# The second block's projections, taken in the first block as pairs of 64-row half tiles

## The chip, the core and the metric

The kernel runs on one core of a Trainium2 chip. A core has five engines that run side by side and wait for each other by semaphores: TensorE (PE, matmuls, its weight loads shown apart as PEld), VectorE (DVE), ScalarE (ACT), GpSimd (POOL) and SyncE (SP, which here only issues DMAs). Sixteen DMA engines move data. The metric is the device time of one execution in microseconds. Before the change it is 217.17 us, the median of 3 runs (216.95 to 217.29).

## What is computed

A sequence of 2048 rows of width 448, normalized once, goes through a sliding-window attention (16 heads of 28, window 256) and, in parallel, through a gated feed-forward part (width 1792). Both results are added to the input.

```python
xn = _layernorm(x)
# attention
q, k, v = split(xn @ wqkv)                 # 16 heads of 28
scores  = q @ k.T * 28 ** -0.5             # masked: 0 <= i - j < 256
a       = softmax(scores) @ v @ wo
# feed-forward
b       = (gelu(xn @ w_gate) * (xn @ w_up)) @ w_down
out     = x + a + b
```

## The kernel before

**Blocks and stages.** The 2048 rows are worked off in four blocks of 512 (`qb` 0 to 3), each of four tiles of 128 rows. A block has an attention stage (`attention`, L560) and a gate stage (`gated`, L451); the down projection of a block (`gen_down`) is done inside the attention stage of the next one. In the first block the attention stage has nine steps (`steps_of`, L502). A step issues four-head score matmuls on PE (`sc`, L632), one exponential over 128x2048 on ScalarE (L638), the masks on GpSimd, and then what its entry in `plan` says. At the start of the steps with index 4, 6 and 8 there is a pass of probabilities times v (`pv`, L591, tile `ov`).

**The plan.** `plan` (L778) is an order written out by hand: a list for each step. `(u, n)` takes n pieces of work from the generator `u`, one piece being between one and seven matmuls; a function is called as it stands. All engines' instructions are issued in this order, each engine works its own off in order, and SP issues its DMAs in this order too. So where a function that issues DMAs stands in the plan decides where these stand on SP.

**What the first block's plan holds.** `gen_qk` makes the first block's own q and k of head groups 1 to 3. `gen_up(0, ...)` makes up-projection pairs 1, 2 and 3 ahead of the gate stage (tile `ue`; a pair is 14 matmuls of 64x512 in seven slots of two at a time, then two casts on VectorE). `gen_v(4, ..)`, `gen_v(6, ..)` and `gen_qk_next` make the second block's v, q and k: six 128-row matmuls and two 64-row halves for each pair of results (`v_dense`, `v_half`, `proj`, `qk_halves`), so 7 slots. `q_last` makes q of head group 3 with four 128-row matmuls. The gate stage begins with up pair 0 (`up(0)`, tile `u`) and gate 0 (tile `gt`).

**Half tiles and swapped copies.** The width of 448 is 3.5 times 128. Up and gate projections, and in blocks 2 and 3 also the projections (`gen_pairs`, L343), use pairs of 64-row matmuls: one on the array's rows 0 to 63, the other on rows 64 to 127, at the same time, seven chunks of 64 each. For every second chunk the data must lie in the other half of the partitions. Three tensors hold such swapped copies: `xsw` of the normalized rows (a ring for two blocks, filled by `swap(qb)`, L409), `wvs` of the v weights and `wsq` of the q and k weights (filled by `swap_weights`, L415). Before, `swap(1)` and both `swap_weights` stand at the start of the second block (L797 to L800), where only the second block's gate stage and the projections for blocks 2 and 3 need them.

**Normalization.** `stat(t)` takes mean and variance of a tile on VectorE, `rstd(t, n)` makes the deviations of n tiles with two small activations on ScalarE, `norm(t)` writes the normalized tile `xn` (448 columns, and again 64 columns as a second copy of the last half chunk) and `dma_transp(t)` transposes it by DMA into `xnT`. For tiles 5, 6 and 7 the 64 columns are GpSimd's (L167). `rstd(5, 3)` stands in the third step right before the exponential, behind that step's q copy (L636).

**Loads.** `ahead()` (first step) transposes tile 4 and loads part of `wu` and `wg`; `ahead3()` (third step) normalizes and transposes tiles 5 to 7 and then, by `loads()`, loads the rest of `wu`, `x_sb`, the rest of `wg`, `wo` and `wd`, all on SP. `fill_pads(False)` in the fourth step completes the weights `wqp` and `wkp` on GpSimd; `wsq` is a copy of these.

**PSUM banks.** Projections, up pairs and `ov` share four banks (`take` and `give`, L203): the one that was given back first is taken next. A bank is free once the copy out of it is done. The scores have a pool of their own.

Of the kernel before, what the change touches and what calls it, by code (L numbers as in the profile page):

```python
# [17 lines left out]
P = 128  # L18
# [8 lines left out]
def kernel(  # L27
# [136 lines left out]
    def norm(t):  # L164
        xn = work.tile([P, 4, P], bf16, name="xn", bufs=4)
        xf = xn[:, :, :].rearrange("p a b -> p (a b)")
        both = ((nc.vector, 0, D, 0), (nc.gpsimd if t in (5, 6, 7) else nc.vector, D, 64, 384))  # L167
        for eng, lo, n, src in both if t > 3 else both[:1]:
            eng.tensor_scalar(out=xf[:, lo:lo + n], in0=x_sb[:, t, src:src + n], scalar1=mv_all[:, t, 0:1],
                              scalar2=rstd_all[:, t:t + 1], op0=ALU.subtract, op1=ALU.mult)  # L170
        xns[t] = xn
# [47 lines left out]
    def v_dense(t, pv):  # L219
        mm3(pv, lambda c: xnT[:, c, t * P:(t + 1) * P], lambda c: wv[:, c, :], True, False)  # L220
# [4 lines left out]
    def v_copy(t, pv, copy):  # L225
        copy(out=v_sb[:, t, :, 0:Dh], in_=pv.rearrange("p (h d) -> p h d", d=Dh))
        give(pv)

    def gen_v(t, scalar):

        two = [None, None]
        for i in range(2):
            two[i] = take("pv", D)
            v_dense(t + i, two[i])
            yield 570
        for i in range(2):
            v_half(t + i, two[i])
        for i in range(2):
            v_copy(t + i, two[i], nc.vector.tensor_copy if i and not scalar else nc.scalar.copy)
        yield 360  # L240

# [81 lines left out]

    def gen_qk_next():

        pairs = []
        for g, parts, end in ((0, "qk", None), (1, "q", 0), (1, "k", None), (3, "", 1), (2, "qk", 2)):
            for part, w in (("q", wqp), ("k", wkp)):
                if part in parts:
                    ps = take("p" + part)  # L330
                    proj(ps, w, 1, g)
                    pairs.append(ps)
                    yield 650
            if g == 3:
                q_last(1)
                yield 870
            if end is not None:
                two, pairs = pairs[:2], pairs[2:]
                qk_halves(1, end, *two)
                qk_copies(1, end, *two)  # L340
                yield 360

    def gen_pairs(qb):  # L343

# [26 lines left out]

        return chain(v_pair(4 * qb), qk_pair(0), v_pair(4 * qb + 2), qk_pair(1), qk_pair(2))

# [186 lines left out]
    def attention(qb, plan):  # L560
# [54 lines left out]
        for i, (scores, ncol, edges) in enumerate(steps):  # L615
# [12 lines left out]
            for g, half, kt, q0, nq, col in scores:  # L628
# [9 lines left out]
            nc.scalar.activation(out=p_sb[:, :, 0:ncol], in_=ss[:, :, 0:ncol], func=ACT.Exp, scale=SCALE)  # L638
# [101 lines left out]
    def ahead():  # L740
        norm(4)
        dma_transp(4)
        load_ffn(wu, B_w_up, slice(0, 1))
        load_ffn(wg, B_w_gate, slice(0, 3))

    def ahead2():
        stat(6)
        stat(7)

    def ahead3():  # L750
        for t in (5, 6, 7):
            norm(t)
            dma_transp(t)
        loads()

    def loads():

        load_ffn(wu, B_w_up, slice(4, 7))
        nc.sync.dma_start(out=x_sb[:, 12:16, :], in_=xv[:, 12:16, :])
        load_ffn(wg, B_w_gate, slice(3, 7))  # L760
        wo_v = A_wo.rearrange("(g j d) n -> j d g n", g=4, j=4)
        for j in range(4):
            nc.sync.dma_start(out=wo[32 * j:32 * j + Dh, :, :], in_=wo_v[j])
        for k in range(0, NF, 4):
            n = min(4, NF - k)
            nc.sync.dma_start(out=wd[:, k:k + n, :], in_=rows(B_w_down, k, n))

    for qb in range(NB):
# [4 lines left out]
        if qb == 0:  # L773
            new_hT(0)
            early = (1, 2, 3)
            u = chain(gen_qk((1, 2, 3), {1: (3, pvs[3]), 2: (2, pvs[2])}), gen_up(0, (1, 2)), gen_v(4, False), gen_up(0, (3,)),
                      gen_v(6, True), gen_qk_next())
            plan = [[(u, 2), ahead, (u, 1)], [lambda: v_dense(2, pvs[2]), (u, 2), ahead2, (u, 1)], [lambda: spare.append(spare.pop(1)), (u, 2), ahead3, (u, 4)],  # L778
                    [(u, 11), lambda: fill_pads(False)], [lambda: stat(8), (u, 10), lambda: fill_pads(True)], [(u, 3)],
                    [lambda: stat(9), (u, 4)], [lambda: stat(10), (u, 3)], [lambda: stat(11), (u, 3), lambda: rstd(8, 4)]]  # L780
        else:
            d = gen_down(qb - 1)
            if qb < 3:
                u = gen_pairs(qb + 1)
                plan = [[(d, 14)], [(d, 11)], [(d, 11)], [(u, 7)], [(d, 18)], ["sums", (u, 7), "inverse"], [(u, 12)],
# [189 lines left out]
```

## Time and profile before

| | us |
|---|---|
| median of 3 runs | 217.17 |
| the profiled execution | 217.4 |
| its span, first to last instruction | 215.7 |
| first block, attention steps (scores of the first to up pair 0) | 11.6 to 37.0 |
| first block, gate stage | 37.0 to 54.8 |
| DMA moved in the span | 15.21 MB |

How to read the lines: a row of the timeline or of the chain has the start in us, the duration in us, engine, source line, operation, output and inputs, and in brackets the idle time before it and what ended it. PE's matmuls overlap, so durations of single ones are longer than the distance of their starts, and the distance tells the rate. A row of SP is the issue of a DMA, not its transfer. A row of waits has who waited for whom, us in total, how often, and the longest. A row of a stretch has its bounds and length, then each engine's busy time with its count, the granted clock, the share of the DMA engines and GB/s.

### The profile page before, as it was taken

To read this page: it belongs to the slowest core of one execution; us is meant where nothing else is said; L and a number is where in the kernel's file an instruction comes from. 1 tells how busy PE (TensorE), PEld (TensorE's weight loads), DVE (VectorE), ACT (ScalarE), POOL (GpSimd) and SP (SyncE) were. 2 spreads that over 40 slices of the span, in tenths; PEclk is the share of its full clock that TensorE was granted. 3 is DMA by queue.
4 is the path that set the end of the run, shared out by engine and by line. 5 is a ranking of instruction groups with operands and counts; after the bars stand their busy time and mean duration, and the time that the engine had idled before them with its cause. 6 is when DMAs were issued, how large, how long until landed. Compare 5 with 4: busy or idle time off the path is not lost.

```text
span 215.7 us, 6281 instructions
## 1 busy us (share of the span) xinstructions
PE 209.6 (97%) x2687; PEld 101.7 (47%) x2692; DVE 156.7 (73%) x348; ACT 132.0 (61%) x125; POOL 48.0 (22%) x81
## 2 busy tenths in 40 slices
PE   7999999999999999999999999999999999999993
PEld 2433333444445445544445445544444444444793
DVE  7896779799456997588547799567359699687721
ACT  4698589645876976613777697423578676467000
POOL 5286968520000202022000012022000020205001
PEclk9999999999999999999999999999999999999999
DMA  6999499913391000102330000200000000000001
GB/s 195 267 241 184 80 231 226 300 30 69 78 251 51 24 3 27 18 3 50 70 97 24 24 0 3 58 9 3 0 3 22 26 3 24 21 3 0 21 29 49
DMA packets 23553, 15.21 MB, mean 71 GB/s; under 512 B 9856, under 2 KB 23264, under 8 KB 23520
## 3 DMA queue, kind: packets, MB, share of 16 engines
q1 hardware_dynamic: 22576, 14.47, 27.9%
q8 instruction: 22, 0.36, 0.6%
q10 hardware_dynamic: 944, 0.29, 0.5%
q14 instruction: 11, 0.09, 0.2%
HBM read 8.69 MB, written 2.18 MB: 50 GB/s over the span
## 4 chain that ended last, share of the span: by engine, by line
PE 92%; DMA 2%; DVE 2%; ACT 1%; issue 1%; POOL 1%; DVEq 0%; POOLq 0%; ACTq 0%
PE po L391 26%; PE gt L431 20%; PE u L431 14%; PE sc L632 6%; PE ue L431 5%; PE ov L599 5%; PE pq L365 4%; PE pv L351 3%; PE pq L190 3%; PE pv L190 2%; PE pk L190 2%; DMA xnT<-xn 1%; DMA x_sb<-in_A_x_dram 1%; ACT p_sb L638 1%; DVE st L154 1%
## 5 line engine op out<-in xcount | busy, mean ns | idle before, releaser
L638 ACT ACTIVATE p_sb<-sc 128x2048 bf16<-128x2048 f32 x39 | 73.3, 1878 | 20.6 <-PE sc L632 13.8
L566 POOL TENSOR_TENSOR oN<-oc,l 128x512 bf16<-128x512 f32 x16 | 22.2, 1387 | 140.3 <-DVE l L579 140.3
L470 ACT ACTIVATE ge<-gt 128x1024 bf16<-128x1024 f32 x28 | 28.7, 1024 | 39.1 <-PE gt L431 33.8
L391 PE MATMUL po<-wd,hT 128*128 128x448 bf16 (+1 forms) x266 | 47.9, 324 | 0.0
L431 PE MATMUL gt<-xnT,wg 64*128 64x512 bf16 x224 | 45.4, 376 | 0.0
L431 PE MATMUL gt<-xsw,wg 64*128 64x512 bf16 x168 | 40.6, 376 | 0.0
L478 DVE TENSOR_TENSOR hT<-ge,u 128x512 bf16<-128x512 bf16 x38 | 24.4, 680 | 17.9 <-PE u L431 10.1
L547 DVE TENSOR_TENSOR p_sb<-p_sb,masks 128x256 bf16<-128x256 bf16 (+1 forms) x90 | 30.1, 390 | 5.9 <-ACT p_sb L638 5.9
L391 PEld LDWEIGHTS <-hT 128*128 128x128 bf16 x266 | 24.6, 98 | 16.0 <-issue 1.0
L431 PE MATMUL u<-xnT,wu 64*128 64x512 bf16 x152 | 31.7, 376 | 0.0
L431 PEld LDWEIGHTS <-wg 64*128 64x128 bf16 x392 | 19.6, 94 | 21.9 <-issue 0.2
L431 PEld LDWEIGHTS <-wu 64*128 64x128 bf16 x392 | 19.0, 94 | 23.0 <-issue 3.3
L431 PE MATMUL u<-xsw,wu 64*128 64x512 bf16 x114 | 27.2, 376 | 0.0
L399 DVE TENSOR_TENSOR res<-po,x_sb 128x448 bf16<-128x448 f32 (+1 forms) x17 | 10.1, 593 | 18.8 <-PE po L391 18.8
L632 PE MATMUL sc<-qT,kT 28*64 28x320 bf16 (+7 forms) x648 | 16.4, 261 | 0.3 <-ACT p_sb L638 0.2
L557 POOL TENSOR_SCALAR_AFFINE_SELECT p_sb<-p_sb 128x512 bf16<-128x512 bf16 (+1 forms) x21 | 14.3, 707 | 4.7 <-ACT p_sb L638 4.6
L431 PE MATMUL ue<-xnT,wu 64*128 64x512 bf16 x72 | 15.1, 377 | 0.0
L391 PE MATMUL po<-wo,oN 128*128 128x448 bf16 (+1 forms) x76 | 15.1, 323 | 0.0
L447 DVE CAST hT<-ue 128x512 bf16<-128x512 f32 x18 | 11.5, 682 | 2.9 <-PE ue L431 2.9
L632 PEld LDWEIGHTS <-kT 28*64 28x64 bf16 (+1 forms) x648 | 7.7, 102 | 12.6 <-issue 10.9
L431 PE MATMUL ue<-xsw,wu 64*128 64x512 bf16 x54 | 13.5, 377 | 0.0
L572 DVE STREAM_TRANSPOSE l<-oc 128x512 f32<-128x512 f32 x16 | 11.3, 704 | 1.6 <-POOL oN L566 1.6
(103 smaller groups left out, 251.7 us busy)
## 6 DMA issues: line engine op xcount, KB each, us to landing
out_dram<-res SPq DMA_DIRECT2D x15, 112.0 KB
xsw<-xnT SPq DMA_DIRECT2D x8, 192.0 KB
x_sb<-in_A_x_dram SPq DMA_DIRECT2D x3, 448.0 KB
wu<-in_B_w_up_dram SPq DMA_DIRECT2D x4, 336.0 KB
wd<-in_B_w_down_dram SPq DMA_DIRECT2D x3, 448.0 KB
wg<-in_B_w_gate_dram SPq DMA_DIRECT2D x2, 448.0 KB
wg<-in_B_w_gate_dram SPq DMA_DIRECT2D x2, 336.0 KB
wraw<-in_A_wqkv_dram SPq DMA_DIRECT2D x2, 252.0 KB
```

Source lines behind the costliest of these rows:

```text
L190: nc.tensor.matmul(ps, lhsT=lhs(c), rhs=rhs(c), start=start and c == 0, stop=stop and c == 2, skip_group_check=True)
L391: nc.tensor.matmul(po[:, a:b], lhsT=x[:, k, cs], rhs=wt[:, k, lo + a:lo + b], start=(n == a == 0), stop=(n == len(terms) - 1), skip_group_ ...
L431: nc.tensor.matmul(ps, lhsT=w[64 * hi:64 * hi + 64, c, p * P:(p + 1) * P], rhs=xchunk(qb, hi, c, qb * QB, QB), start=c == 0, stop=c == 6, ...
L447: nc.vector.tensor_copy(out=hTs[qb][:, p + 7 * i, :], in_=us[i])
L470: nc.scalar.activation(out=ges[p][:, :, :], in_=gt[:, :, :], func=ACT.Gelu_apprx_tanh)
L478: nc.vector.tensor_tensor(out=hT[:, p + 7 * i, :], in0=ge[:, i, :], in1=u, op=ALU.mult)
L547: nc.vector.tensor_tensor(out=reg, in0=reg, in1=m, op=ALU.mult)
L557: nc.gpsimd.affine_select(out=reg, in_=reg, pattern=mid + [[1 if diag else -1, min(w, P)]], compare_op=ALU.is_ge, fill=0.0, base=0 if diag ...
L566: nc.gpsimd.tensor_tensor(out=oN[:, g, :], in0=oc[:, :], in1=inv, op=ALU.mult)
L572: nc.vector.transpose(out=l1[:, :, :].rearrange("p a b -> p (a b)"), in_=oc[:, :])
L632: nc.tensor.matmul(ss[k0:k0 + nk, j, col:col + nq], lhsT=kT[r, g, kt * P + k0:kt * P + k0 + nk], rhs=qT[r, g, ring(qb).start + q0:ring(qb) ...
L638: nc.scalar.activation(out=p_sb[:, :, 0:ncol], in_=ss[:, :, 0:ncol], func=ACT.Exp, scale=SCALE)
```

## The change

Five things are changed in the first block; blocks 1 to 3 keep their own plans.

- The second block's v, q and k come from `gen_pairs(1, ...)`, that is from half-tile pairs, in the order v, v, q/k of groups 0, 1 and 2; `gen_v` and `gen_qk_next` are gone. `q_last(1)` moves to the ninth step.
- Up pair 0 joins the pairs made early, in the fifth step; the projections start in the sixth.
- The 64 columns of `xn` are VectorE's for all tiles.
- `rstd(5, 3)` stands in `ahead2()`, in the second step, ahead of the third step's q copy.
- The swapped copies come earlier: `wvs` is loaded from DRAM in `ahead()`, `swap(1)` stands in `ahead3()` behind the transposes, and `swap_weights()` (for `wsq`) at the head of `loads()`, which now is called in the fourth step, behind `fill_pads(False)`, and holds `wo` and `wd`.

```diff
     def norm(t):
...
-        both = ((nc.vector, 0, D, 0), (nc.gpsimd if t in (5, 6, 7) else nc.vector, D, 64, 384))
-        for eng, lo, n, src in both if t > 3 else both[:1]:
-            eng.tensor_scalar(out=xf[:, lo:lo + n], in0=x_sb[:, t, src:src + n], scalar1=mv_all[:, t, 0:1],
+        both = ((0, D, 0), (D, 64, 384))
+        for lo, n, src in both if t > 3 else both[:1]:
+            nc.vector.tensor_scalar(out=xf[:, lo:lo + n], in0=x_sb[:, t, src:src + n], scalar1=mv_all[:, t, 0:1],
...
-    def gen_v(t, scalar):
...
-    def gen_qk_next():
...
-    def gen_pairs(qb):
+    def gen_pairs(qb, order):
...
-        return chain(v_pair(4 * qb), qk_pair(0), v_pair(4 * qb + 2), qk_pair(1), qk_pair(2))
+        return chain(*(v_pair(4 * qb + n) if kind == "v" else qk_pair(n) for kind, n in order))
...
-    def swap_weights(dst, *srcs):
-
-        for hi, src in enumerate(srcs):
-            nc.sync.dma_start(out=dst[64 * hi:64 * hi + 64], in_=src[64 - 64 * hi:P - 64 * hi, 0:3])
+    def swap_weights():
+
+        for hi, src in enumerate((wqp, wkp)):
+            nc.sync.dma_start(out=wsq[64 * hi:64 * hi + 64], in_=src[64 - 64 * hi:P - 64 * hi, 0:3])
...
-            if not qb and i == 2:
-                rstd(5, 3)
...
     def ahead():
         norm(4)
         dma_transp(4)
+        wv64 = A_wqkv[0:3 * P, 2 * D:3 * D].rearrange("(c h p) n -> h p c n", h=2, p=64)
+        for hi in range(2):
+            nc.sync.dma_start(out=wvs[64 * hi:64 * hi + 64, :, :], in_=wv64[1 - hi])
         load_ffn(wu, B_w_up, slice(0, 1))
         load_ffn(wg, B_w_gate, slice(0, 3))
 
     def ahead2():
         stat(6)
         stat(7)
+        rstd(5, 3)
 
     def ahead3():
         for t in (5, 6, 7):
             norm(t)
             dma_transp(t)
-        loads()
-
-    def loads():
-
+        swap(1)
         load_ffn(wu, B_w_up, slice(4, 7))
         nc.sync.dma_start(out=x_sb[:, 12:16, :], in_=xv[:, 12:16, :])
         load_ffn(wg, B_w_gate, slice(3, 7))
+
+    def loads():
+
+        swap_weights()
         wo_v = A_wo.rearrange("(g j d) n -> j d g n", g=4, j=4)
...
-            early = (1, 2, 3)
-            u = chain(gen_qk((1, 2, 3), {1: (3, pvs[3]), 2: (2, pvs[2])}), gen_up(0, (1, 2)), gen_v(4, False), gen_up(0, (3,)),
-                      gen_v(6, True), gen_qk_next())
-            plan = [[(u, 2), ahead, (u, 1)], [lambda: v_dense(2, pvs[2]), (u, 2), ahead2, (u, 1)], [lambda: spare.append(spare.pop(1)), (u, 2), ahead3, (u, 4)],
-                    [(u, 11), lambda: fill_pads(False)], [lambda: stat(8), (u, 10), lambda: fill_pads(True)], [(u, 3)],
-                    [lambda: stat(9), (u, 4)], [lambda: stat(10), (u, 3)], [lambda: stat(11), (u, 3), lambda: rstd(8, 4)]]
+            early = (0, 1, 2, 3)
+            u = chain(gen_qk((1, 2, 3), {1: (3, pvs[3]), 2: (2, pvs[2])}), gen_up(0, (1, 2, 3, 0)))
+            w = gen_pairs(1, (("v", 0), ("v", 2), ("k", 0), ("k", 1), ("k", 2)))
+            plan = [[(u, 2), ahead, (u, 1)], [lambda: v_dense(2, pvs[2]), (u, 2), ahead2, (u, 1)],
+                    [lambda: spare.append(spare.pop(1)), (u, 2), ahead3, (u, 4)], [(u, 11), lambda: fill_pads(False), loads],
+                    [lambda: stat(8), (u, 14), lambda: fill_pads(True)], [(w, 7)], [lambda: stat(9), (w, 10)],
+                    [lambda: stat(10), (w, 7)], [lambda: stat(11), lambda: q_last(1), (w, 11), lambda: rstd(8, 4)]]
...
-        if qb == 1:
-            swap_weights(wvs, wv, wv)
-            swap_weights(wsq, wqp, wkp)
-            swap(1)
```

More of the change, by code (lines that the diff above doesn't have):

```diff
@@ L227, in v_copy @@
         give(pv)
-    def gen_v(t, scalar):
[L231 to L240, printed above, removed]
     def proj(ps, w, qb, g):
@@ L322, in deliver @@
             nc.sync.dma_start(out=kT[32 * j:32 * j + Dh, 3, qb * QB:(qb + 1) * QB], in_=k3[j].rearrange("t i n -> (t i) n"))
-    def gen_qk_next():
[L326 to L341, printed above, removed]
-    def gen_pairs(qb):
+    def gen_pairs(qb, order):
         def v_pair(t):
@@ L783 @@
             if qb < 3:
-                u = gen_pairs(qb + 1)
+                u = gen_pairs(qb + 1, (("v", 0), ("k", 0), ("v", 2), ("k", 1), ("k", 2)))
                 plan = [[(d, 14)], [(d, 11)], [(d, 11)], [(u, 7)], [(d, 18)], ["sums", (u, 7), "inverse"], [(u, 12)],
```

2 lines of the change are left out of this document (1 added, 1 removed).

## The prediction

> **What bounds the kernel now.** I read the page from the top: busy times, the tenths of the 40 slices, the chain of waits by engine.
>
> ```profile
> PE 209.6 (97%) x2687; PEld 101.7 (47%) x2692; DVE 156.7 (73%) x348; ACT 132.0 (61%) x125; POOL 48.0 (22%) x81
> PEclk9999999999999999999999999999999999999999
> DMA  6999499913391000102330000200000000000001
> PE 92%; DMA 2%; DVE 2%; ACT 1%; issue 1%; POOL 1%; DVEq 0%; POOLq 0%; ACTq 0%
> ```
>
> TensorE (PE) is the bound: busy for 97% of 215.7 us, with 92% of the chain. A change gains only by closing gaps on PE, and every gap that it opens is paid in full. The DMA row matters as much here: slices 1 to 3 and 5 to 7 (5.4 to 21.6 us and 27 to 43 us) are full, so a transfer put there stands in a line.
>
> The change works between 13 and 38.5 us, in the first block's attention. The chain of waits in order of time, and PE's timeline, show what can be won there:
>
> ```profile
> 21.02 0.61 POOL xn L169 x2
> 21.63 2.87 DMA xnT<-xn
> 24.55 0.74 PE pv L190 x3
> ```
> ```profile
> 19.23 0.38 PE L431 MATMUL ue<-xsw,wu 64*128 64x512 bf16 x1
> 19.77 0.40 PE L632 MATMUL sc<-qT,kT 28*128 28x128 bf16 x8 [0.17 <-ACT p_sb L638]
> 23.52 0.74 PE L190 MATMUL pv<-wv,xnT 128*128 128x448 bf16 x3
> 33.19 0.81 PE L190 MATMUL pq<-xnT,wqp 128*128 128x512 bf16 x3
> 33.83 0.38 PE L266 MATMUL pq<-xnT,w3p 128*128 128x512 bf16 x1
> 34.15 0.39 PE L196 MATMUL pq<-xnT,w3p 64*128 64x512 bf16 x1
> ```
>
> Three 512-column matmuls take 33.83 - 33.19 = 0.64 us from start to start, 0.213 each: one slot. From a 128-row matmul to 64-row halves it is 0.32 (33.83 to 34.15), so a change of tile costs 0.1. Now the gaps. From 19.23 to 19.77 are 0.54, a slot and a change of tile explain 0.31: 0.23 is the wait for the exponential. The three matmuls from 23.52 issue in 0.57 (0.213 x 448/512 each), the next starts at 24.55: 0.46 is the wait for tile 5's transpose, which waited for GpSimd.
>
> **What the change may gain.** The deviations move ahead of a q copy:
>
> ```profile
> 16.94 0.59 ACT L256 CAST qT<-pq 128x512 bf16<-128x512 f32 x1 [0.59 <-PE pq L196]
> 17.42 0.30 ACT L159 ACTIVATE lnv<-mv_all,eps_t 128x3 f32<-128x3 f32 x1
> 17.86 1.86 ACT L638 ACTIVATE p_sb<-sc 128x2048 bf16<-128x2048 f32 x1
> 17.99 1.01 DVE L169 TENSOR_SCALAR xn<-x_sb,mv_all,rstd_all 128x448 bf16<-128x448 bf16 x3
> ```
>
> They fill ScalarE's 0.59 of idleness, the exponential starts some 0.35 earlier, and the 0.23 goes. On VectorE three 64-column pieces join the 1.01 us of normalization: under 0.2 each, by the 0.34 of a 448-column one. They delay only group 3's k copy, whose user is four steps on. xn of tile 5 is whole at about 18.5 instead of 21.63. The 0.46 goes, since the second block's first projection moves behind up pair 0, a step later. The projections as half-tile pairs keep the number of slots (v: 6 dense + 1 pair = 7 pairs; q and k likewise) and save the change of tile in four of five groups (q_last keeps one): 0.4. Up pair 0 moves with its 7 slots; its two casts replace work after gate 0, on a VectorE that is 73% busy. Together -1.1 us, if all data come in time.
>
> **What it moves on the queue.** The half-tile pairs read the swapped copies xsw, wvs and wsq. Before, these were loaded at the second block's start; now they stand in the first block's line on SP (SyncE's queue):
>
> ```profile
> 14.92 1.30 SPq L81 DMA_DIRECT2D wu<-in_B_w_up_dram  x2
> 16.27 1.30 SPq L81 DMA_DIRECT2D wg<-in_B_w_gate_dram  x2
> 21.63 4.39 SPq L175 DMA_TRANSPOSE xnT<-xn  x3
> 26.07 1.28 SPq L81 DMA_DIRECT2D wu<-in_B_w_up_dram  x2
> 28.06 1.28 SPq L81 DMA_DIRECT2D wg<-in_B_w_gate_dram  x2
> ```
> ```profile
> 38.81 0.38 SPq L766 DMA_DIRECT2D wd<-in_B_w_down_dram  x1
> SPq L766 <- DMA wg<-in_B_w_gate_dram: 3.4, 2, 1.8
> ```
> ```profile
> 16.20:21.60 5.40, 5.23 (x48) 1.95 (x49) 3.53 (x9) 4.76 (x7) 3.63 (x7) 1.00 1.03 183
> 27.00:32.40 5.40, 5.35 (x60) 2.13 (x59) 4.23 (x9) 4.62 (x5) 3.46 (x7) 1.00 0.95 234
> 32.40:37.70 5.30, 5.25 (x56) 2.04 (x51) 5.16 (x11) 5.30 (x6) 4.47 (x8) 1.00 1.13 224
> 37.70:43.00 5.30, 5.30 (x66) 2.36 (x64) 3.96 (x8) 3.49 (x6) 2.95 (x4) 1.00 1.06 306
> ```
> ```profile
> xsw<-xnT SPq DMA_DIRECT2D x8, 192.0 KB
> wvs<-wv SPq DMA_DIRECT2D x2, 168.0 KB
> wsq<-wqp SPq DMA_DIRECT2D x1, 192.0 KB
> wsq<-wkp SPq DMA_DIRECT2D x1, 192.0 KB
> ```
>
> The last numbers of a stretch's row are the share of the DMA engines and GB/s. SP issues in order and shares eight completion counters: a DMA cannot be issued until the eighth before it has landed. That dates a landing: the last wd load went out at 38.81, released by the second half of the wg load issued from 28.06. So a load issued at about 28.7 landed at 38.8. It stood behind 672 KB of wu, 448 KB of x and the first 448 KB of wg; with itself 2.06 MB, and the rows moved 5.4 x 234 + 5.3 x 224 + 1.1 x 306, or 2.8 MB, up to 38.8 (of which some are the first wo and wd). The line is served in order, late ones last.
>
> Now the new line. Behind tile 4's transpose: wvs (2 issues), wu, wg, the transposes of tiles 5 to 7, xsw (waits for those four transposes), wu, x, wg, and then, in the fourth step, wsq, wo, wd. Its times:
> - wvs puts 1.35 of issue ahead: the transposes start at 18.97, not at 18.5, and their 4.39 end at 23.4. Its 344 kB take 1.9 us at 183 GB/s of a full line, so that the first wg ends at 23 or later, and the transposes' data behind it. A transpose moves 131 kB, 0.7 at 183 GB/s. Tile 7's landing: between 24.1 (the 23.4 and its own 0.7) and 25.7 (all 1.9 added to the 21.6 at which the full slices ended, and three times 0.7); I take 25.0.
> - xsw: issued from 25.1, the second half from 25.75; priced with the 2.87 from issue to landing of a transpose, it is there at 28.6. PE wants it at 26.7, for the v pair of the sixth step. Stall 1.9.
> - wu follows at 26.45 instead of 26.07; with the old 12.7 from there (26.07 to 38.8) the last wg lands at 39.15. That xsw's 393 kB lie in front adds 0 to 1.7; I take 0, as the line needs over a microsecond to start anyway.
> - wsq is next: 393 kB at 224 to 306 GB/s, 1.3 to 1.75. I take 1.65; it lands at 40.8 (39.5 to 43.3 with all bounds). Its first user is the second matmul of group 0's q/k pair, in the seventh step. From 28.6 PE has two v pairs of 7 x 0.19, a pv pass of 0.67 and a score step of 0.40 (rows below): it gets there at 32.4 and stands for 8.4 us. Behind that matmul in PE's order are all remaining scores of the block, and then everything.
>
> **From the landing to gate 0.**
>
> ```profile
> 29.83 0.82 PE L190 MATMUL pq<-xnT,wqp 128*128 128x512 bf16 x2
> 32.20 0.40 PE L632 MATMUL sc<-qT,kT 28*128 28x384 bf16 x8
> 34.47 0.67 PE L599 MATMUL ov<-p_sb,v_sb 128*32 128x256 bf16 x16
> 37.03 0.38 PE L431 MATMUL u<-xnT,wu 64*128 64x512 bf16 x1
> 38.54 0.38 PE L431 MATMUL gt<-xnT,wg 64*128 64x512 bf16 x1
> ```
> ```profile
> 32.78 1.88 ACT L638 ACTIVATE p_sb<-sc 128x2048 bf16<-128x2048 f32 x1
> 34.55 0.59 ACT L268 CAST qT<-pq 128x512 bf16<-128x512 f32 x1
> 1.38 3.92 PE L149 MATMUL wps<-wo 128*128 128x512 bf16 x9 [1.38 <-DVE wo L123]
> ```
>
> Before, the same 25 slots, two score steps and one pv pass took 37.03 - 29.83 = 7.2; two changes of tile fewer make it 7.0. The new order adds two waits for a PSUM bank (four banks, handed out first in, first out). A q copy that now stands behind an exponential frees its bank 0.58 + 1.88 + 0.59 = 3.05 after that step's scores (32.20 to 32.78, and the two durations). The third pv pass takes the bank of group 0's q, whose copy is behind the eighth step's exponential; PE comes to it after 0.33 + 7 slots, 2.0: wait 1.1. Group 2's k takes the bank of q_last, copied behind the ninth's; PE is there after 2.25: wait 0.8. Gate 0's exponential-table load now follows at once on the last copies: 0.1 on gate 2. That is 9.0. Last, the clock: at the start PE comes from idleness and 9 matmuls of 512 columns take 3.92, 0.436 each, twice a slot. After 8 us of idleness I expect that again, 2.0 us more; 1.1 of it covers the first bank wait. So 9.9, and 8.9 to 9.9 as bounds.
>
> The Trainium skill, "TensorE: Matmul & The Clock Gate", Part 1, gives a rule for this: after an idle window of about 3.4 us the array's clock falls to half and returns only after about as long a busy one. The start's row agrees; no row here shows a fall in mid-kernel.
>
> **The sum**, against the profiled execution (217.4, span 215.7 and 1.7 around it, 0.2 above the median of 217.17): gate 0 at 40.8 + 9.9 + 0.1 = 50.8 instead of 38.54. Up pair 0, 1.5 before, is no longer ahead of it, which that difference holds. From there on the work is the same and PE is full: +12.3, that is 229.7 in the profile's terms and **229.5** by the median.
>
> **Rivals.**
> - The clock stays up: -0.9, 228.6. For it: the granted clock is 9 in every slice, in the first one too, where the 9 matmuls were slow; so that row does not show what slowed them.
> - wsq overtakes the loads, or is served in turns with them: only xsw is late. PE at group 0 at 32.4, +9.0 = 41.4, +2.9: 220. Against it: the landing at 38.8 of a load issued at 28.7.
> - The line is longer: all upper bounds (25.7 for tile 7, 1.7 for xsw), 232 to 233.
> - The other side: xsw lands before 26.7 and wsq before 30.4, and the bank waits hide in VectorE's copies; then the -1.1 stands: 216.1. It decides at wsq's landing: each microsecond after 30.4 costs one. It needs 10 us less than the line shows.
>
> **Numbers.** Forecast 0.60; clock up 0.17; wsq in turns 0.09; longer line 0.08; the faster side 0.04; no effect, the two cancelling, 0.02. The range, 226.5 to 232.5, holds the first two with the bounds of the landing (-1.3, +2.5). Within 0.2%, 0.4 us, a difference cannot be told from none. Faster 0.04, same 0.02, slower 0.94.
>
> **What would show it.** Right: in the changed profile a gap on PE of 7 to 10 us ending near 41, released by the DMA into wsq; a smaller one near 28 released by xsw; after the long one some 3 to 4 us of 512-column matmuls 0.43 apart; the gates then as before. Wrong: pk matmuls on wsq at 31 to 33 without a wait, or wsq landing before wg.

## The result, and the profile after

| | before | after |
|---|---|---|
| median (4 runs each, in turns on one chip) | 217.23 us | 231.56 us |
| ratio, 95% interval | | 1.066 (1.064 to 1.068) |
| the profiled execution | 217.4 us | 231.59 us |
| its span | 215.7 us | 229.9 us |
| start of gate 0 | 38.54 us | 52.21 us |

The forecast was 229.5 us, with 226.5 to 232.5 around it. The kernel became slower by 14.2 us of span. From the page of the profile after: busy times, and the chain of waits by engine:

```profile
PE 214.5 (93%) x2722; PEld 103.0 (45%) x2722; DVE 160.7 (70%) x355; ACT 130.8 (57%) x122; POOL 46.4 (20%) x78
PE 74%; ACT 6%; DVE 6%; DMA 6%; POOL 4%; issue 3%; SPq 0%; ACTq 0%; DVEq 0%; POOLq 0%
```

PE's busy time grew by 4.9 us (209.6 to 214.5), the span by 14.2: the rest is idleness. Its share of the chain of waits fell from 92% to 74%, and 6% of the chain are now DMA. PE's waits, each with the total, the count and the longest:

```profile
PE pk L333 <- DMA wsq<-wkp: 5.8, 1, 5.8
PE pv L319 <- DMA xsw<-xnT: 3.2, 1, 3.2
PE pk L333 <- ACT qT L255: 0.4, 1, 0.4
PE ov L567 <- ACT qT L243: 0.3, 1, 0.3
```

These are the four waits of the forecast: wsq, xsw, and two PSUM banks. The timeline of SP's issues, two of SP's waits and PE's timeline place them:

```profile
17.70 1.30 SPq L81 DMA_DIRECT2D wg<-in_B_w_gate_dram  x2
19.10 5.01 SPq L175 DMA_TRANSPOSE xnT<-xn  x3
26.78 1.28 SPq L381 DMA_DIRECT2D xsw<-xnT  x2
31.45 0.91 SPq L386 DMA_DIRECT2D wsq<-wqp  x1
39.24 3.91 SPq L737 DMA_DIRECT2D wd<-in_B_w_down_dram  x4
SPq L737 <- DMA wg<-in_B_w_gate_dram: 4.0, 2, 2.3
SPq L737 <- DMA wsq<-wkp: 0.3, 1, 0.3
```
```profile
26.86 0.36 PE L319 MATMUL pv<-wv,xnT 64*128 64x448 bf16 x1
30.45 0.56 PE L319 MATMUL pv<-wvs,xsw 64*128 64x448 bf16 x2 [3.23 <-DMA xsw<-xnT]
36.59 0.38 PE L333 MATMUL pq<-xnT,wqp 64*128 64x512 bf16 x1
42.81 0.60 PE L333 MATMUL pk<-xsw,wsq 64*128 64x512 bf16 x1 [5.84 <-DMA wsq<-wkp]
```

Read the two side by side. xsw's issue waits for the transposes, so 26.78 dates the landing of tile 7. PE begins the first v pair at 26.86 and has its second matmul, the first with xsw, only at 30.45. It reaches group 0's q/k pair at 36.59, does one matmul, and stands until 42.81. The wd loads, issued from 39.24 on, wait first for the two halves of wg and only then for wsq, so wsq landed behind wg. The windows of that stretch (length, PE's busy time with its count, granted clock, DMA share, GB/s) show a thing that the forecast had for the second wait only:

```profile
27.20:30.40 3.20, 0.02 (x1) 0.77 0.66 140
30.40:35.50 5.10, 5.05 (x41) 0.50 1.10 257
35.50:37.00 1.50, 1.47 (x13) 0.91 1.07 196
37.00:42.80 5.80, 0.00 (x0) 0.69 1.08 238
42.80:46.00 3.20, 3.19 (x20) 0.50 1.08 328
46.00:52.20 6.20, 5.49 (x60) 1.00 0.20 67
```

A mean of 0.77 over 3.20 us is 1.5 us at half clock, so the clock fell at 28.9, still inside the first wait; by the same reckoning it came back at 35.8, fell again at 39.2 and came back at 46.0. PE's work ran at half clock for 5.3 us behind the first wait and for 3.2 behind the second. The first of these should have cost nothing, since PE had to wait for wsq afterwards anyway.

### The profile page after: what moved, and what is told of

The parts are those of the page before. It is cut to its first block, busy times and chain, and to the rows that moved or that the text cites. A ratio compares the mean times of both kernels' runs of the same rounds, so it can differ in the third digit from the quotient of the medians.

```text
span 229.9 us, 6344 instructions
## 1 busy us (share of the span) xinstructions
PE 214.5 (93%) x2722; PEld 103.0 (45%) x2722; DVE 160.7 (70%) x355; ACT 130.8 (57%) x122; POOL 46.4 (20%) x78
## 4 chain that ended last, share of the span: by engine, by line
PE 74%; ACT 6%; DVE 6%; DMA 6%; POOL 4%; issue 3%; SPq 0%; ACTq 0%; DVEq 0%; POOLq 0%
PE po L359 25%; PE gt L399 14%; PE u L399 11%; PE sc L600 5%; DMA wsq<-wkp 4%; PE ue L399 4%; PE pq L333 4%; PE ov L567 4%; ACT p_sb L604 3%; PE pv L319 3%; POOL p_sb L525 2%; DVE st L154 2%; PE pk L333 1%; DVE xn L169 1%; DMA x_sb<-in_A_x_dram 1%
## 5 line engine op out<-in xcount | busy, mean ns | idle before, releaser
L446 DVE TENSOR_TENSOR hT<-ge,u 128x512 bf16<-128x512 bf16 x36 | 23.2, 681 | 18.0 <-PE u L399 10.3
L399 PE MATMUL u<-xnT,wu 64*128 64x512 bf16 x144 | 30.0, 376 | 0.0
L399 PE MATMUL u<-xsw,wu 64*128 64x512 bf16 x108 | 25.8, 376 | 0.2 <-DVE hT L446 0.2
L525 POOL TENSOR_SCALAR_AFFINE_SELECT p_sb<-p_sb 128x512 bf16<-128x512 bf16 (+1 forms) x21 | 14.2, 701 | 19.1 <-ACT p_sb L604 19.0
L333 PE MATMUL pk<-xsw,wsq 64*128 64x512 bf16 x27 | 10.9, 404 | 6.2 <-DMA wsq<-wkp 5.8
L399 PE MATMUL ue<-xnT,wu 64*128 64x512 bf16 x80 | 16.6, 377 | 0.0
L399 PE MATMUL ue<-xsw,wu 64*128 64x512 bf16 x60 | 14.9, 377 | 0.0
L415 DVE CAST hT<-ue 128x512 bf16<-128x512 f32 x20 | 12.8, 683 | 1.2 <-PE ue L399 1.2
```

The lines of the kernel that those rows point to most:

```text
L333: nc.tensor.matmul(ps, lhsT=w.rearrange("p h d -> p (h d)"), rhs=xchunk(qb, hi, c, qb * QB, QB), start=c == 0, stop=c == 6, tile_position= ...
L399: nc.tensor.matmul(ps, lhsT=w[64 * hi:64 * hi + 64, c, p * P:(p + 1) * P], rhs=xchunk(qb, hi, c, qb * QB, QB), start=c == 0, stop=c == 6, ...
L415: nc.vector.tensor_copy(out=hTs[qb][:, p + 7 * i, :], in_=us[i])
L446: nc.vector.tensor_tensor(out=hT[:, p + 7 * i, :], in0=ge[:, i, :], in1=u, op=ALU.mult)
L525: nc.gpsimd.affine_select(out=reg, in_=reg, pattern=mid + [[1 if diag else -1, min(w, P)]], compare_op=ALU.is_ge, fill=0.0, base=0 if diag ...
```

## The experiments

All times are medians of several runs, set against runs of the kernel before on the same chip (217.1 to 217.3). A version builds on the one named. Gate 0's start is that of one execution each, and these lie 0.1 to 0.2 us apart from the first scores on, so a difference below that says nothing. The executions shown of four versions lie 0.5 to 0.6 us above their medians: the first, q copies on VectorE, the normalization alone, and half tiles for q and k only. Sizes are in KB of 1024 bytes, as the views have them; the 393 and 344 kB of the recorded texts are 384 and 336 KB.

| version | us | ratio to before, 95% interval | gate 0 |
|---|---|---|---|
| wsq ahead of the bulk loads | 223.3 | 1.025 (1.021 to 1.028) | 44.13 |
| and the transposes ahead of wg | 219.86 | 1.012 (1.010 to 1.013) | 40.71 |
| and q copies on VectorE | 219.33 | 1.009 (1.008 to 1.011) | 40.41 |
| before, with the change's normalization alone | 217.02 | 0.999 (0.998 to 1.000) | 38.68 |
| the change, with filler matmuls | 230.04 | 1.059 (1.057 to 1.060) | 50.62 |
| transposes ahead, group 0 whole | 218.86 | 1.007 (1.006 to 1.009) | 39.59 |
| and q of group 3 first | 218.27 | 1.004 (1.002 to 1.005) | 38.87 |
| and wvs behind the transposes | 218.76 | 1.007 (1.005 to 1.008) | 39.18 |
| q of group 3 first, copies moved | 218.23 | 1.004 (1.003 to 1.005) | 38.68 |
| before, with up pair 0 early | 217.48 | 1.001 (1.000 to 1.002) | 38.86 |
| half tiles for q and k only | 217.41 | 1.002 (1.001 to 1.003) | 39.01 |
| and group 0 dense | 217.47 | 1.001 (1.000 to 1.002) | 38.37 |

### Is it the place of wsq in the line?

```diff
     def ahead3():
...
         swap(1)
-        load_ffn(wu, B_w_up, slice(4, 7))
-        nc.sync.dma_start(out=x_sb[:, 12:16, :], in_=xv[:, 12:16, :])
-        load_ffn(wg, B_w_gate, slice(3, 7))
     def loads():
         swap_weights()
+        load_ffn(wu, B_w_up, slice(4, 7))
+        nc.sync.dma_start(out=x_sb[:, 12:16, :], in_=xv[:, 12:16, :])
+        load_ffn(wg, B_w_gate, slice(3, 7))
```

> Theory: the second wait is the place of wsq in SP's line, behind 2 MB of loads. With wsq's two copies put right behind xsw (issued near 28.1, 1.4 us of issue, about 3 from issue to landing) it lands near 32, before TensorE asks at 36.6. The 5.8 us wait and the slow matmuls after it go; gate 0 moves from 52.4 to 36.6 + 9.0 = 45.6, the time from 231.6 to about 224.8 (223.5 to 226). The wait for xsw (3.2) stays. Rival, the half-tile pairs and their bank waits cost the time whatever the line does: less than 2 us won, 229.5 or more.

Measured: 223.3. PE's waits and SP's issue of xsw in its profile:

```profile
PE pv L319 <- DMA xsw<-xnT: 3.1, 1, 3.1
```
```profile
26.58 1.28 SPq L381 DMA_DIRECT2D xsw<-xnT  x2
```

No wait for wsq is left, and nothing but the order of issues was changed: 8.3 us of the 14.3 came from 2.0 MB of loads (672 KB of wu, 448 of x, 896 of wg) that stood ahead of 384 KB. The wait for xsw is as it was, and the clock falls behind it here too, which now costs time:

```profile
27.10:30.30 3.20, 0.10 (x1) 1.00 0.74 180
30.30:35.00 4.70, 4.68 (x45) 0.64 1.03 238
```

These are the windows of that wait and behind it; the third number from the end is the granted clock. A mean of 0.64 over 4.70 us is 3.4 us at half. Of the four executions behind the median one kept its clock (a mean of 1.000 over the span, the others 0.991 or 0.992): it took 221.48 us, the others 223.22 to 223.94. So this fall costs some 1.9 us, a wait of 3.1 us doesn't always bring it, and without it, by that one execution, the order of issues is worth 10 us. The bank wait in front of the third pv pass shows its full size (0.9), as no slow matmuls cover it.

### Is the rest of the line the transposes?

```diff
     def ahead():
...
-        load_ffn(wg, B_w_gate, slice(0, 3))
     def loads():
         swap_weights()
+        load_ffn(wg, B_w_gate, slice(0, 3))
```

> As the run before, and the first wg load is moved from ahead of the transposes of tiles 5 to 7 to behind wsq. Theory: the transposes came late because they stood behind that load in a full line. Now tile 7 lands near 23.5 to 24.5 instead of 26.6, xsw near 27, wsq near 29.5; no wait of TensorE for a DMA over 0.5 us, no slow matmuls after 6 us. What is left are the two bank waits (up to 1.9 at full clock) against gains of 1.1: 218.0 (217.0 to 219.0). Rival, the transposes are late by themselves (issue, VectorE's order): tile 7 still lands after 26, xsw near 30, time near 223.

Measured: 219.86, above what was expected. SP's issues, and PE's timeline:

```profile
18.80 4.45 SPq L175 DMA_TRANSPOSE xnT<-xn  x3
24.66 1.28 SPq L381 DMA_DIRECT2D xsw<-xnT  x2
```
```profile
28.46 0.36 PE L319 MATMUL pv<-wvs,xsw 64*128 64x448 bf16 x2 [1.17 <-DMA xsw<-xnT]
35.86 0.67 PE L567 MATMUL ov<-p_sb,v_sb 128*32 128x256 bf16 x16 [0.92 <-ACT qT L243]
39.40 0.37 PE L333 MATMUL pk<-xsw,wsq 64*128 64x512 bf16 x1 [0.39 <-ACT qT L255]
```

The transposes are issued 0.3 us earlier than in the changed kernel, and tile 7 is there 2.1 us earlier (24.66 against 26.78; 26.58 in the experiment before). So 1.6 to 1.8 of it was the wg load of 672 KB that stood right ahead of them. Without that load three transposes still take 5.9 us from the first issue to the landing of the last (18.80 to 24.66): 4.45 of issue and 1.4 behind it, where the forecast had reckoned 4.4 and 0.7. That is why 1.2 us of waiting for xsw stay. After 1.17 us of idleness the clock did not fall, after the 3.1 of the version before it did in three executions of four.

### Are the bank waits ScalarE's?

```diff
-            qk_copies(qb, g, *two, nc.vector.tensor_copy if g == 1 else nc.scalar.copy)
+            qk_copies(qb, g, *two, nc.vector.tensor_copy if g == 1 or qb == 1 and g == 0 else nc.scalar.copy)
...
-                    [lambda: stat(10), (w, 7)], [lambda: stat(11), lambda: q_last(1), (w, 11), lambda: rstd(8, 4)]]
+                    [lambda: stat(10), (w, 7)], [lambda: stat(11), lambda: q_last(1, nc.vector.tensor_copy), (w, 11), lambda: rstd(8, 4)]]
```

> As the run before, and the q copies of group 0 and of q_last for the second block go from ScalarE to VectorE, where no exponential stands ahead of them. Theory: the two bank waits (near the third pv pass and at group 2's k) go and the 1.1 of gains stand: 216.1 (215.5 to 217.0), 1 to 2 us below the run before. Rival, VectorE's queue makes these copies as late (0.7 each on an engine with transposes and sums in those steps): within 0.5 us of the run before.

Measured: 219.33, a miss: 216.1 was expected, and within 0.5 us of the 219.86 if VectorE makes the copies as late. The second bank wait is gone; the first is not, PE now waits 1.1 us there for VectorE's q copy. VectorE's timeline:

```profile
34.70 0.58 DVE L154 BATCH_NORM_STATS2 st<-x_sb 128x6 f32<-128x448 bf16 x1
35.41 0.66 DVE L243 CAST qT<-pq 128x512 bf16<-128x512 f32 x1
```

Group 0's pair ends in the eighth step, PE's last matmul of it ends at 35.06, and the third pv pass, which takes its bank, comes right behind it. So PE waits for the whole copy, 0.66 us, on either engine; the statistics of a later tile, which stand ahead of the copy on VectorE, add the 0.35 from 35.06 to 35.41. The wait is one of place in the order more than of an engine.

### Does the normalization gain what it was priced at?

The kernel before, with two edits of the change:

```diff
-        both = ((nc.vector, 0, D, 0), (nc.gpsimd if t in (5, 6, 7) else nc.vector, D, 64, 384))
+        both = ((nc.vector, 0, D, 0), (nc.vector, D, 64, 384))
...
-            if not qb and i == 2:
-                rstd(5, 3)
...
     def ahead2():
         stat(6)
         stat(7)
+        rstd(5, 3)
```

> The kernel before with two parts of the change alone: the deviations in the second step, and the 64 columns of tiles 5 to 7 on VectorE. Theory: the exponential's 0.23 is won; the transposes are issued near 18.6, right behind the first wg load in a full line, and land little before the 24.5 of before: 0.2 to 0.5 won, 216.7 to 217.0. If the line did not hold them, tile 5 would land near 21.5 and 0.69 would be won: 216.5. Rival, VectorE pays for the moved pieces: no change or slower.

Measured: 217.02, 0.1% faster. SP's row, and the first projection on PE:

```profile
18.83 4.79 SPq L175 DMA_TRANSPOSE xnT<-xn  x3
```
```profile
24.70 0.74 PE L190 MATMUL pv<-wv,xnT 128*128 128x448 bf16 x3 [0.45 <-DMA xnT<-xn]
```

The transposes are issued 2.8 us earlier (18.83 instead of 21.63), and PE waits for tile 5 as before, 0.45 instead of 0.29: what it won at the exponential it gives back here. GpSimd's 64 columns were the releaser in the chain of waits, but 2.8 us of earlier issue bought nothing at the landing. What held the transposes then is, by the experiment on their place, the wg load right ahead of them; this kernel wasn't run without it.

### What does the clock cost?

The changed kernel, with matmuls in the two waits whose results nobody reads:

```diff
+    def filler(n):
+        tag = spare[0]
+        ps = take("fill")
+        for _ in range(n):
+            nc.tensor.matmul(ps, lhsT=ident[:, :], rhs=xnT[:, 0, 0:QB], start=True, stop=True, skip_group_check=True)
+        held.pop(id(ps))
+        spare.insert(0, tag)
...
-                    [(w, 7)], [lambda: stat(9), (w, 10)],
+                    [lambda: filler(14), (w, 7)], [lambda: stat(9), (w, 7), lambda: filler(36), (w, 3)],
```

> The changed kernel as it is, plus matmuls whose results nobody reads: 14 of 128x128x512 ahead of the second block's first v pair and 36 ahead of group 0's q/k pair. They fill most of the two waits (for xsw, 3.2 us, and for wsq, 5.8 us) and nothing else. Theory (the half clock is TensorE's answer to idleness): with TensorE busy up to the landing of wsq, the 512-column matmuls behind it come 0.21 apart instead of 0.42, the stretch from the landing to gate 0 shrinks by what of the 2 us isn't covered by the bank wait, some 0.6 to 0.9 us, and the time is 230.7 (230.3 to 231.1). Rival (the slow matmuls have another cause, such as weights that have just landed): still 0.42 apart behind the landing, 231.6.

Measured: 230.04, a little more won than the 230.3 to 231.1 expected. Its windows and PE's timeline:

```profile
30.40:35.50 5.10, 5.05 (x58) 1.00 1.10 262
42.10:46.00 3.90, 2.98 (x40) 1.00 1.07 330
```
```profile
42.08 0.39 PE L341 MATMUL pk<-xsw,wsq 64*128 64x512 bf16 x1
```

The clock stays at 1.00 with the same loads in the line: PE's idleness is what makes it fall. From wsq to gate 0 are 50.62 - 42.08 = 8.5 us instead of 52.21 - 42.81 = 9.4, so the clock cost 0.9, the 2.0 less the 1.1 that the forecast let the bank wait cover. The other 0.7 is wsq, which was there by 42.08 in this execution; how much of that is the filler and how much one execution against another isn't settled.

### How much of the rest are the remaining waits?

From the version with the transposes ahead, first the plan, so that group 0's q copy stands ahead of the eighth step's exponential:

```diff
-                    [lambda: stat(8), (u, 14), lambda: fill_pads(True)], [(w, 7)], [lambda: stat(9), (w, 10)],
-                    [lambda: stat(10), (w, 7)], [lambda: stat(11), lambda: q_last(1), (w, 11), lambda: rstd(8, 4)]]
+                    [lambda: stat(8), (u, 14), lambda: fill_pads(True)], [(w, 7)], [lambda: stat(9), (w, 14)],
+                    [lambda: stat(10), (w, 7)], [lambda: stat(11), lambda: q_last(1), (w, 7), lambda: rstd(8, 4)]]
```

> The version with wsq and the transposes ahead of the bulk loads (219.9), with the plan alone changed: the whole q/k pair of group 0 (14 pieces instead of 10) in the seventh step, so that ScalarE's q copy stands ahead of the eighth step's exponential and not behind it. Theory (the third pv pass waits 1.0 us for the PSUM bank of that copy because of this order): the wait goes, 218.9; as group 2's k pair begins one step on as before, its wait of 0.5 for the bank of q_last stays or shrinks: 218.4 to 219.1. Rival (the bank wait only covers lateness of an engine that sets the pace anyway, so another wait appears): 219.5 to 219.9.

Then `q_last(1)` moved to the head of the sixth step:

> As the one before, and q of head group 3 moves from the ninth step to the sixth, ahead of the first v pair. It reads no swapped copy, only the transposed rows, so its 0.96 us of matmuls cover most of the 1.2 us in which TensorE stands for xsw (landing at 28.4, v pair's second matmul then at 28.0), and its bank is long free when group 2's k wants it. Theory (the three remaining waits are all that keeps this version above the kernel before; without them gate 0 would start at 38.0, 0.5 before that kernel's): gate 0 at 38.3 to 38.5, time 217.2 (216.8 to 217.6). Rival (something else is slower by the half-tile pairs themselves, a chunk rate or the casts on VectorE): 218 or more with no wait of over 0.3 left in the sixth to ninth step.

Then the load of `wvs` moved from `ahead()` to just ahead of `swap(1)`:

> As the one before, and the load of wvs moves from ahead of the transposes of tiles 5 to 7 to behind them, just ahead of xsw. Theory (the changed kernel's transposes lost their time to loads that were still in the line when they were issued): the transposes are issued 0.8 to 1.3 earlier, tile 7 lands 1 to 2 us earlier than the 24.5 of the version with the transposes ahead, so at 22.5 to 23.5, and xsw, now behind 344 kB of wvs, at 27 to 28.4; no wait for xsw is left, 217.0 (216.7 to 217.3). Rival (what slows the transposes is their own work, not the loads): tile 7 lands as much earlier as it is issued, 0.8 to 1.3, and wvs costs xsw that again: 217.2 to 217.8.

Measured: 218.86, 218.27 and 218.76. The first bank wait went, as expected, for 1.0 us. q of group 3 covered the wait for xsw; what is left in that version, by PE's waits:

```profile
PE pk L333 <- DVE qT L243: 0.6, 1, 0.6
PE pv L319 <- DMA xsw<-xnT: 0.3, 1, 0.3
```

Its gate 0 starts at 38.87, where 38.3 to 38.5 was expected, and it is 1.1 us above the kernel before though gate 0 is 0.33 late. So something is lost behind gate 0 too. The third version is a miss, 0.5 us slower than the one it builds on, with 0.6 of waiting for xsw. SP's issues, and those of a later version that loads wvs last of all (half tiles for q and k only):

```profile
18.71 4.49 SPq L175 DMA_TRANSPOSE xnT<-xn  x3
24.68 1.27 SPq L381 DMA_DIRECT2D xsw<-xnT  x2
```
```profile
18.62 4.92 SPq L175 DMA_TRANSPOSE xnT<-xn  x3
24.80 1.28 SPq L394 DMA_DIRECT2D xsw<-xnT  x2
```

With no wvs ahead of them the transposes are issued at 18.71 and have landed by 24.68, the same as with it (18.80 and 24.66). Here xsw's issue stands behind that of wvs, which ends at 24.5, so this row alone couldn't show an earlier landing; the later version can, and has 24.80. So in these versions the issue waited for VectorE's normalization, not for wvs, and with wg out of the way the 336 KB of wvs, two loads ahead of the transposes, did not slow them. Whether wvs adds to the delay that wg makes, no run takes apart: in the trace the packets of the transposes (256 bytes each) end at 26.0 in the changed kernel, with both loads in front, and at 25.0 in the run with the normalization alone, with wg and without wvs.

### Where is the loss behind gate 0?

From the version with q of group 3 first, q copies moved between the engines and the deviations moved ahead of group 2's pair:

```diff
-            qk_copies(qb, g, *two, nc.vector.tensor_copy if g == 1 else nc.scalar.copy)
+            qk_copies(qb, g, *two, nc.vector.tensor_copy if g == (2 if qb == 1 else 1) else nc.scalar.copy)
...
-                    [lambda: stat(10), (w, 7)], [lambda: stat(11), (w, 7), lambda: rstd(8, 4)]]
+                    [lambda: stat(10), (w, 7), lambda: stat(11)], [lambda: rstd(8, 4), (w, 7)]]
```

> The version with q of group 3 first (218.3), with three things moved between engines: in the second block's projections group 1's q copy goes to ScalarE, group 2's to VectorE, and the deviations of tiles 8 to 11 stand ahead of group 2's pair (their last statistics one step earlier). Theory (what is left above the kernel before is two waits: 0.57 us of TensorE for the bank of group 1's q copy, which VectorE makes late, and the first gelu, which starts 2.5 us after gate 0 instead of 1.7, as the activation table can only be loaded behind the last copy and up pair 0 no longer stands in between): the bank wait goes, the table load comes some 0.3 us earlier against gate 0, 217.4 (217.1 to 217.7). Rival (VectorE, now with one copy more behind the last pair, is late for the first products and gives it back): 218.0 to 218.4.

And the kernel before, with `gen_up(0, (1, 2, 0))`, `early = (0, 1, 2, 3)` and 17 pieces instead of 10 in the fifth step:

> The kernel before, with one part of the change alone: up pair 0 made in the fifth step, ahead of the second block's first projection, instead of ahead of gate 0. Theory (up pair 0 ahead of gate 0 gave ScalarE the 1.5 us that the last copies and the table load need): TensorE no longer waits 0.46 for tile 5's transpose, so gate 0 starts at 38.0 to 38.2 instead of 38.5, but the first gelu starts 2.3 to 2.7 us after it instead of 1.7, and what was won is given back in the gate stage: 217.0 to 217.5. Rival (the table load hides behind gates anyway): 216.6 to 216.8.

Measured: 218.23 and 217.48. First the start of the gate stage on ScalarE, before and after:

```profile
38.41 1.28 ACT L803 ACT_TABLE_LOAD   x1
40.26 1.02 ACT L470 ACTIVATE ge<-gt 128x1024 bf16<-128x1024 f32 x1 [0.56 <-PE gt L431]
45.52 1.02 ACT L470 ACTIVATE ge<-gt 128x1024 bf16<-128x1024 f32 x1 [0.46 <-PE gt L431]
```
```profile
53.44 1.28 ACT L771 ACT_TABLE_LOAD   x1
54.73 1.02 ACT L438 ACTIVATE ge<-gt 128x1024 bf16<-128x1024 f32 x1
59.62 1.02 ACT L438 ACTIVATE ge<-gt 128x1024 bf16<-128x1024 f32 x1 [0.74 <-DVE hT L443]
```

Before, the table load is done before gate 0 is, and gelu waits for PE. After, the first gelu follows the table load, 2.5 us after gate 0 instead of 1.7. VectorE's first product follows that gelu, the fourth gelu waits for one of VectorE's products, and so 0.43 of the delay is left there: 13.67 late at the first gate, 14.10 at the fourth gelu. Now the two experiments, ScalarE and PE of the first, then PE of the second:

```profile
40.40 1.02 ACT L438 ACTIVATE ge<-gt 128x1024 bf16<-128x1024 f32 x1
46.30 1.02 ACT L438 ACTIVATE ge<-gt 128x1024 bf16<-128x1024 f32 x1 [1.12 <-DVE hT L443]
```
```profile
38.68 0.37 PE L399 MATMUL gt<-xnT,wg 64*128 64x512 bf16 x1 [0.35 <-ACT p_sb L604]
```
```profile
38.86 0.37 PE L431 MATMUL gt<-xnT,wg 64*128 64x512 bf16 x1 [0.34 <-ACT p_sb L638]
```

Neither went as its theory had it. In the first the bank wait went and gelu came earlier against gate 0 (1.7 behind it), but the fourth comes 7.6 us behind gate 0 (7.4 in the changed kernel, 7.0 before): VectorE, with the copies behind the last pair, gives it back, as the rival said. And both show a wait that was on no list: gate 0 takes a score bank, and that is free only when the ninth step's exponential has read it. Before, up pair 0 stood between the last scores and gate 0 and covered that exponential. With up pair 0 early and nothing else in between, gate 0 cannot start before the last exponential ends. In the second experiment PE's wait for tile 5 is gone, as foreseen, but the gain of 0.3 to 0.5 that was expected at gate 0 turned into a loss of 0.3, of which up to 0.2 may be the execution's own offset. Its fourth gelu comes 7.0 us behind gate 0 as before, so nothing more was lost in the gate stage: its time came out as foreseen by luck.

### Is there a version that beats both?

From the version with q of group 3 first: up pair 0 back ahead of gate 0, v from 128-row matmuls, q of group 3, then the three q/k pairs as half tiles, with all their q copies on ScalarE; wvs loaded last:

```diff
-            early = (0, 1, 2, 3)
-            u = chain(gen_qk((1, 2, 3), {1: (3, pvs[3]), 2: (2, pvs[2])}), gen_up(0, (1, 2, 3, 0)))
-            w = gen_pairs(1, (("v", 0), ("v", 2), ("k", 0), ("k", 1), ("k", 2)))
+            early = (1, 2, 3)
+            u = chain(gen_qk((1, 2, 3), {1: (3, pvs[3]), 2: (2, pvs[2])}), gen_up(0, (1, 2, 3)), gen_v(4, False), gen_v(6, True))
+            w = gen_pairs(1, (("k", 0), ("k", 1), ("k", 2)))
...
-                    [lambda: stat(8), (u, 14), lambda: fill_pads(True)], [lambda: q_last(1), (w, 7)], [lambda: stat(9), (w, 14)],
+                    [lambda: stat(8), (u, 10), lambda: fill_pads(True)], [(u, 3), lambda: q_last(1)], [lambda: stat(9), (w, 7)],
```

> A version that keeps of the change only what the runs so far didn't speak against: up pair 0 stays ahead of gate 0 as in the kernel before, the second block's v is made of 128-row matmuls as before (so wvs isn't needed early and is loaded last), q of group 3 follows, and only the q/k pairs of groups 0 to 2 are half-tile pairs, with xsw and wsq loaded behind the transposes and ahead of all bulk loads. With VectorE's normalization, the earlier deviations and all q copies of these pairs on ScalarE. Theory (every loss found so far is a wait for late data, a late copy, or gate 0's cover, and none lies in the half-tile pairs): xsw lands by 28 and wsq by 30, TensorE comes to the first q/k pair at 30.4 to 30.8; the waits of 0.2 and 0.46 us and three changes of tile of 0.1 go, gate 0 at 37.7 to 38.0 instead of 38.5, time 216.5 (216.2 to 216.9). Rival (the end of the first block's attention is set by the last exponential and the copies behind it, which do not move): 217.0 to 217.4.

Then group 0's q and k from 128-row matmuls as well:

> As the version before (217.4), with one change: group 0's q and k of the second block are made of 128-row matmuls as in the kernel before, so only groups 1 and 2 are half-tile pairs, and wsq, which landed at 31.4 there while TensorE came at 30.2 and lost 1.0 us, is first wanted at 33. Theory (that wait was all that hid the gain): gate 0 at 37.9 to 38.1 instead of the 38.5 of the kernel before, nothing given back behind it since up pair 0 covers the table load, time 216.4 to 216.7. Rival (the end of the attention stage is set elsewhere, by the exponentials and the copies): 217.0 to 217.4.

Measured: 217.41 and 217.47. A row of PE's timeline of each:

```profile
31.48 0.39 PE L346 MATMUL pk<-xsw,wsq 64*128 64x512 bf16 x1 [0.87 <-DMA wsq<-wkp]
```
```profile
32.46 0.40 PE L623 MATMUL sc<-qT,kT 28*128 28x384 bf16 x8 [0.32 <-ACT p_sb L627]
```
The first, in an execution 0.5 us above its median, lost 0.9 to wsq, which was there at 31.4 and not by 30. In the second that is gone, and 0.3 of what was saved went into a wait of the eighth step's scores for the seventh's exponential; its gate 0 is 0.17 us earlier than in the kernel before, too little to say anything. Both missed their theories (216.5) and came out where the rivals had them, 0.1 to 0.2% above the kernel before: there was no gain. Of all versions only the one with the normalization alone, 217.02, lies below the kernel before, by 0.1%.

## Why the prediction was right

The mechanism was the one forecast: swapped copies queued behind bulk loads, TensorE standing in front of xsw and then, far longer, of wsq; the first two experiments took 11.7 of the 14.3 us away by the order of issues alone. Step by step:

- **The possible gain, -1.1.** Only the 0.23 appeared: in the changed kernel's timeline the fourth step's scores start without the wait for the exponential that they had before.

```profile
19.66 0.40 PE L600 MATMUL sc<-qT,kT 28*128 28x128 bf16 x8
```

  The 0.46 for tile 5's transpose was not GpSimd's: with GpSimd out of the way the transpose landed no earlier. The wait does go where up pair 0 is made early, as forecast, but there 0.34 of it came back as the wait in front of gate 0. Of the 0.4 for changes of tile no time shows anything; in the last version a wait for the seventh step's exponential took back a part.
- **Tile 7 at 25.0 (24.1 to 25.7).** This is the term that was mis-sized: 26.78, outside its bounds. The transposes' start was right, 19.10 for 18.97. The way from there to the last landing was 7.7 us, where 5.1 and a part of wvs's 1.9 were reckoned. Two things were too small: three transposes alone take 5.9, and having the wg load right ahead of them adds 1.6 to 1.8. The forecast had put the delay to wvs pushing wg; wvs alone makes none, and how much of the 1.6 to 1.8 it has a part in stays open.
- **xsw at 28.6.** 30.45. From issue to use it took 30.45 - 26.78 = 3.7, where 28.6 - 25.1 = 3.5 was reckoned; the other 1.7 are tile 7's. PE's wait for it was 3.2 us, not 1.9, and it brought the clock down, which was not forecast.
- **The wait for wsq, 8.4 (a sign: 7 to 10).** 5.8. PE came to it at 36.59 instead of 32.4: xsw was 1.9 later, and the 3.8 us of work behind it took 6.1, most of it at half clock. The time doesn't show this miss, since it goes from wsq's landing on.
- **wsq at 40.8 (39.5 to 43.3).** 42.8. The loads ahead of it went out behind xsw, at 26.78 + 1.28 = 28.1 instead of 26.45, which is 1.6 of the 2.0, and it was served behind them, as the rows of wd's issue and waits show. The rival by which it is served in turns with the loads (220) fell with this row.
- **From the landing to gate 0, 9.9 (8.9 to 9.9).** 9.4. The bank waits of 1.1 and 0.8 are there, at full clock 0.92 and 0.39. The clock fell as forecast and came back after 3.2 us, and its price of 0.9 is the one that the filler showed. That row settles the rival with the clock up (228.6).
- **0.1 for the table load.** 0.5, the other mis-sized term: the first gelu came 0.8 later behind gate 0, and VectorE's products passed 0.43 of it on. That up pair 0 had also covered the last exponential, only the two experiments with a wait in front of gate 0 show. (The sum has this 0.1 twice, in the 9.0 and again at the end.)

The sum by these measures is 13.67 at gate 0, of which 2.0 are the later landing and -0.6 the shorter way from it (12.3 + 2.0 - 0.6 = 13.7), and 0.5 behind gate 0: 14.2.

The rule that the forecast cited, the Trainium skill's "TensorE: Matmul & The Clock Gate", Part 1, agrees with these runs in kind: the clock went to half around waits of 3.1 us and more, not after 1.17, and came back behind a stretch of work. In length it fits less well. In the changed kernel the fall came at 28.9, 1.7 us after the end of PE's last matmul (27.2), and the return took 3.2 us of work behind the long wait, but 5.3 behind the short one.

## What to carry to other kernels

A layout copy by DMA is priced by what stands ahead of it in its queue, not by its own bytes: put small transfers with a near user ahead of bulk loads with a late one, and check what stands right ahead of transposes. Before work is taken out from between two stages, list everything that it covers on the other engines (an activation table load, a bank that is still being read, copies), as the gap on the bound engine is only one of them. When one wait is removed, the gain is no more than the distance to the next one, and in a kernel that is 97% full that distance was a few tenths of a microsecond.

## What the runs showed of the hardware

- DMA transposes were held by ordinary loads issued right ahead of them on the same queue: with 672 KB of wg in front the last of three landed 7.7 us after the first issue (19.10 to 26.78), without it 5.9 (18.80 to 24.66). 336 KB of wvs ahead of wu made no difference where wg was out of the way. Two windows follow, of the changed kernel and of the version without wg in front; the last two numbers are the share of the DMA engines, which counts the whole time of every packet that starts in the window and so can pass 1, and GB/s. With wg in front the engines are more than taken up and yet move only 143 GB/s, against 257 in the window from 30.40. Without it they are not full, and 4.45 of the 5.9 us are SP's three issues.

```profile
22.00:24.00 2.00, 2.00 (x40) 0.86 (x38) 1.78 (x4) 0.47 (x1) 1.95 (x5) 1.00 2.18 143
22.00:24.00 2.00, 2.00 (x40) 0.91 (x38) 1.78 (x4) 0.46 (x2) 1.88 (x4) 1.00 0.64 128
```

- The granted clock fell to 0.50 in the middle of the kernel, with waits of 3.1 us (three executions of four), 3.2 and 5.8, and 14 and 36 matmuls whose results nobody reads kept it at 1.00. By the windows it was at half from 28.9 to 35.8 and from 39.2 to 46.0 in the changed kernel, 6.8 to 6.9 each with 3.4 in between, and for 3.4 in the first experiment: steps of 3.4 us or twice that. This would fit a clock that is set anew every 3.4 us by how busy PE was, so that the same wait brings a fall or not by where it lies against these steps; no run tests that.
